# A planned attention and scan kernel on one core: idle matmuls, longer GpSimd pieces, another rule for late fills, and new seeds

## The chip, the cores and the metric

The kernel runs on one core of a Trainium2 chip. Its engines each follow a list of instructions of their own and meet at semaphores: TensorE (PE) multiplies matrices into eight PSUM banks of 128x512 fp32, ScalarE (ACT) evaluates functions, VectorE (DVE) and GpSimd (POOL) do elementwise work, and SyncE (SP) issues most of the transfers. The metric is the device time of one execution in microseconds (us); smaller is better.

## The reference

Two layers of 2048 tokens by 640 channels, their outputs side by side (2048 x 1280, bf16):

```python
# A: a diagonal complex state space model
Lam = Lambda_re + 1j * Lambda_im;  dt = exp(log_dt);  Lam_bar = exp(dt * Lam)
B_bar = ((Lam_bar - 1.0) / Lam)[:, None] * Bmat
Bu = einsum("bld,pd->blp", x, B_bar)
for t in range(L):  h = Lam_bar * h + Bu[:, t]
y = 2.0 * einsum("blp,dp->bld", hseq, Cmat).real + x * Dskip
# B: attention, 32 heads of 20 channels that share one key and one value head
q = heads(x @ wq);  k = x @ wk;  v = x @ wv
p = softmax(q k^T * 20 ** -0.5)
out = merged(p v) @ wo
```

## The kernel before

**Attention.** The work is cut into 32 groups: 4 blocks of 512 queries by 8 groups of four heads. A group has 4 heads x 16 blocks of 128 keys, so 64 *units*; a unit is a block of 128 keys by 512 queries of one head, and there are 2048 of them. For each unit PE multiplies keys with queries into one PSUM bank (a *fill*, `QK`), an engine takes the exponential, and PE multiplies the result with the values and adds it to the group's sums in the bank PV (`pv`). Sums leave PV at the end of a group by a VectorE copy (`raw_op`, line 1307, tile OTr). Softmax's denominator is a column of ones among the values; it divides later, in `dense_ops` on GpSimd and, for the last two groups, in `norm_last`.

**Two engines for the exponential.** ACT takes tiles of three or two units: PSUM tile R0 has three banks, R1 two, and fills alternate between them, so even tiles are mostly three wide and odd ones two (`ex_op`, line 1263, output P). VectorE takes single units, the *D units*: `dx_op` (line 1269) turns scores into the bits of a bf16 number by an addition to int16 (tile Pd), and `sh_op` (line 1274) makes three shifted copies of it, for up to three units at a time; the average of four shifted versions comes near to the exponential. A D unit's scores lie in one of two banks B0 and B1, which it shares with all background work, or in the third bank of R0 (named R0c), which is lent to it; then the even tile is two wide.

**Background work** is given in threads of operations: the queries of later blocks (`qt`), the state space model (`sa` the products B x and their rotation, `su` and `sr` the scan and its rotation on GpSimd and VectorE, `sy` the output y), the constants of C (`sc`), the normalisation (`dense`), and the output projection (`proj`). In `sc`, lines 852 to 862: per block of C's rows, GpSimd multiplies in five pieces of 128 columns into the fp32 buffer ctmp (line 858), twice, and VectorE makes CGre and CGim of it (line 860).

**The planner.** No order is written out by hand: `main` builds it when the program is made, from a clock per engine and an estimated duration per operation. In each step it collects candidates (a fill, an exponential, a D unit, a shift, a `pv`, the head of each thread), takes the one that would begin first, with a bias and some noise, and appends it to the list of its engine with the waits that it needs. Fill n may be placed once fill n - 2's exponential is placed. A background or `pv` operation on PE that would end later than the next fill could begin, plus an allowed lateness, is put behind the fill:

```python
t_fill = p.begin("pe", o.reads, o.writes)
t_fill = (t_fill, t_fill + self.after[n % 2])
...
if t < t_fill[0] and tl + o.occ * self.pace(tl) + 0.106 * (o.kind != p.pe_kind) > t_fill[1]:
    k = max(k, t_fill[0] + 0.01)
```

`self.after` is a pair: a short lateness of 0.1 to 0.2 us and a long one of 0.35 to 0.5. Where PE would idle for more than SPARE inside a group and has been thinly used, the planner puts in matmuls that add zeros to PV (kind `zero`, from the tile cs). The planner counts matmuls at double time when PE's use over the last 3.4 us is under COLD (`pace`, `load`).

**Seeds.** The units are cut into 64 turns, and at each turn `vary` draws a dozen parameters (among them `after`, the limits for D units, and noise) from the random generator with that turn's seed in SEEDS. So a change of an estimate or a seed gives another order from there on.

**The start.** `setup` loads x transposed, makes the rotation tables and the keys, and leaves a list `rest` on which `main` begins: VectorE's copies of keys 1024 to 2047 from the B banks (tiles KT), the value projection on PE into PV (80 matmuls), and VectorE's copies into VP. No `pv` may be placed before `rest` is empty; fills and exponentials may. `owner` says which thread holds each B bank.

Of the kernel before, what the change touches and what calls it, by code (L numbers as in the profile page):

```python
# [9 lines left out]
ALU = mybir.AluOpType  # L10
# [233 lines left out]
class _Kernel:  # L244
# [7 lines left out]
    QUOTA = 16  # L252
    AGE = 4.0
    DLAST = 58
    SPARE = 0.33
    WINDOW, BUSY, COLD = 3.4, 0.46, 0.36

    SLACK, SLOW = dict(dve=0.15, pool=1.0), dict(pool=1.0)
# [3 lines left out]


    TURNS = 64
    SEEDS = (19006, 20002, 21006, 22006, 23001, 24003, 25001, 26002, 27008, 28003, 0, 30006, 31008, 32005, 33006,
# [4 lines left out]

    def __init__(self, nc, t):
        self.nc, self.t = nc, t
# [544 lines left out]
    def scan_ops(self):  # L817

        K, NC = self, self.NC
        sc, NGRE, NGIM, GRE, GIM = K.sc, self.NGRE, self.NGIM, self.GRE, self.GIM  # L820
        t = self.t
# [11 lines left out]
        ct = [f"tm{i}{h}" for i in (4, 5, 6) for h in self.PIECES]  # L833
# [18 lines left out]
        for c in range(NC):  # L852
            cr, ci = K.Craw[c][:, 0, :], K.Craw[c][:, 1, :]
            keys = [f"Craw{c}0", f"Craw{c}1", "sc"] + (["ostage0", "ostage1"] if c == 4 else ws)
            for (dst, x, y, gx, gy, op, nm) in ((K.CGre, cr, ci, GRE, GIM, ALU.subtract, "CGre"),
                                                (K.CGim, ci, cr, NGRE, NGIM, ALU.add, "CGim")):
                for i in range(0, 640, 128):
                    pool(lambda e, y=y, c=c, gy=gy, i=i: e.tensor_scalar(K.ctmp[:, i:i + 128], y[:, i:i + 128], sc[:, gy, c:c + 1],  # L858
                                                                         None, op0=ALU.mult), keys, [f"ct{i}"] + ct * (i == 0), 128)
                dve(lambda e, dst=dst, x=x, op=op, c=c, gx=gx: e.scalar_tensor_tensor(  # L860
                    out=dst[:, c, :], in0=x, scalar=sc[:, gx, c:c + 1], in1=K.ctmp, op0=ALU.mult, op1=op),
                    keys + ct + [f"ct{i}" for i in range(0, 640, 128)], [nm], 695)
# [264 lines left out]
    def main(self):  # L1127
        K, p = self, self.p
# [8 lines left out]
        begun = [[False] * 4 for _ in range(NG)]  # L1137
# [4 lines left out]
        tiles = deque()  # L1142
# [21 lines left out]
        rest = self.rest  # L1164
# [4 lines left out]
        threads = [("rest", rest), ("norm", norm), ("dense", dense), ("proj", proj), ("qt", qt), ("qr", qr), ("sy", sy), ("sa", sa), ("su", su), ("sr", sr), ("sc", sc_), ("sx", sx), *fins]  # L1169
        owner = ["rest", "rest", None]  # L1170
        rest[-1].done = lambda: owner.__setitem__(slice(0, 2), [None, None])
        holds, since = {}, {}

        def bank(o):

            f = [i for i in range(2) if owner[i] is None]
            if not f:
                return None
            return min(f, key=lambda i: p.begin("pe", (), (f"B{i}",)))
# [50 lines left out]
        def want_d(g, t, n_tile, lent=False):  # L1230
            if not (g > 0 or taken[g] >= 24) or d_group(g) is None:
                return False
            if dunit_left.get(cur["d"] - self.DUNITS, 0):
                return False
            if lent:
                return (self.lend < 9 and owner[2] is None and t_left() and backlog(t) <= self.backlog - 0.5 * n_tile - self.lend
                        and p.begin("pe", (), ("R0c",)) <= t + self.spared[n_tile])
            if bank(None) is None:
                return False
            if any(owner[:2]) and any(t - x > self.starved[name] * (name != "qt" or len(self.qsent) > 0) for name, x in since.items()):  # L1240
                return False
            return (backlog(t) <= self.backlog - 0.5 * n_tile
                    and p.begin("pe", (), (f"B{bank(None)}",)) <= t + self.spared[n_tile])
# [68 lines left out]
        while True:  # L1312
            if self.units * self.TURNS // NU > turn:
                turn = self.units * self.TURNS // NU
                self.vary(self.SEEDS[min(turn, self.TURNS - 1)])
            cand = []
# [4 lines left out]
            def offer(kind, o, bias, thread=None, arg=None):  # L1321
                cand.append((p.begin(o.eng, *o.keys(), o.accum) + bias + self.noise * self.rng.random(), len(cand), kind, o, thread,
                             arg))

            t_fill = None
            early = bool(rest) and any(self.NKC - len(x) >= 8 for x in left[0])
            if cur["fill"] < cur["act"] + 2 and any(x < 64 for x in taken) and not early:
                n = cur["fill"]
                g = next(i for i in range(NG) if taken[i] < 64)
                if g in qt_done:  # L1330
                    t = p.begin("pe", (), (f"R{n % 2}",))
                    size, x = self.TILES[n % 2] - (n % 2 == 0 and owner[2] is not None), bank(None)
                    d = want_d(g, t, n % 2)
                    if not d and size == 3 and want_d(g, t, 0, True):
                        size, d, x = 2, True, 2
                    out, d = pick(size, d)
                    o = fill_op(n, out, d, x)
                    t_fill = p.begin("pe", o.reads, o.writes)
                    t_fill = (t_fill, t_fill + self.after[n % 2])
                    offer("fill", o, -self.noise, arg=(out, d, x))  # L1340
                    t = p.clock["pe"]
                    if d is None and want_d(g, t, 2):
                        d = pick(0, True)[1]
                        if d:
                            offer("fill", fill_op(n, [], d, bank(None)), 0.2, arg=([], d, bank(None)))
            full = bool(tiles) and tile_left.get(tiles[0][0] - self.PTILES, 0) > 0
            if tiles:
                n, out = tiles[0]
# [4 lines left out]
            if shifts:  # L1353
                o = sh_op(*shifts[0])
                t = p.begin(o.eng, *o.keys()) + p.PRE["dve"]
# [4 lines left out]
            if g < NG and g <= cur["raw"] and not rest:  # L1360
                n, whole = ready(g)
# [8 lines left out]
            for name, th in threads:  # L1370
                if not th:
                    continue
                o = th[0]
# [6 lines left out]
                if o.lock:  # L1380
                    i = bank(o)
# [19 lines left out]
            if t_fill is not None:  # L1401
                for i, (k, m, kind, o, name, arg) in enumerate(cand):
                    if o.eng == "pe" and (kind != "fill" or not arg[0]):
                        t = p.begin("pe", *o.keys(), o.accum)
# [4 lines left out]
            _, _, kind, o, name, arg = min(cand, key=lambda x: x[:2])  # L1409
# [4 lines left out]
            if o.eng == "pe":  # L1414
                g, t = cur["pv"], p.begin("pe", *o.keys(), o.accum)
                while (g < NG and any(begun[g]) and any(due[g]) and t - p.clock["pe"] > self.SPARE
                       and self.load(t) < self.BUSY):
                    self.go(self.mms([self.m1(K.PV[:, :], zeros, K.cs[:, 0, 0, :], False, False)],
                                     ["VP", "cosT"], ["PV"], accum=True, kind="zero"))
            self.go(o)  # L1420
            if kind == "bg":
                th = dict(threads)[name]
# [8 lines left out]
            elif kind == "fill":  # L1431
                out, d, x = arg
                self.units += len(out) + (d is not None)
                if out:
                    n = cur["fill"]
# [14 lines left out]
            elif kind == "ex":  # L1450
                n, out = tiles.popleft()
# [17 lines left out]
            elif kind == "sh":  # L1469
                us, i = shifts.popleft()  # L1470
# [60 lines left out]
```

## Time and profile before

| what | value |
|---|---|
| runs | 769.84, 770.16, 772.17 us (median 770.16) |
| the profiled execution | 770.28 us, of which the span from first to last instruction is 768.6 |
| ACT, line 1263 | 677 instructions, 733.1 us busy |
| DVE, line 1269 | 363 D units from the B banks 245.5 us, 73 from R0c 49.9 us |
| DVE, line 1274 | 513 shifts, 260.2 us |
| PE, line 421 (all matmuls) | 704.8 us |
| POOL, line 858 | 50 pieces, from 75.8 to 161.1 us |
| HBM | 9.21 MB read, 12.69 MB written: 28 GB/s over the span |

How to read it: all matmuls are recorded by one helper, so all have line 421, and tiles tell them apart: `R<-QT,KT` and `B<-QT,KT` are fills, `PV<-P,VP` and `PV<-Pd,VP` the products with the values, `PV<-WO,xbT` the value projection, `R<-WO,OTd` and `R<-WO,OTp` the last output projections. The record of an exponential begins while the one before still ends, so durations of one kind sum to more than the time in which ACT was busy. Busy times of PE are modelled.

### The profile page before, as it was taken

Reading aid. Unit: us, or ns where it says so; the run is one execution under the profiler, and the core shown is the slowest. Engines: PE = TensorE matmul, PEld = TensorE weight load, DVE = VectorE, ACT = ScalarE, POOL = GpSimd, SP = SyncE. Lnnn points to the kernel's source line nnn. Section 1 sums busy time; section 2 is a strip of 40 time slices with the busy share of each in tenths; the row PEclk is TensorE's granted clock in tenths of the full one; section 3 lists DMA queues with packets and bytes.
Section 4 is the critical chain, followed back from the end, with each engine's and each line's share of the span. In section 5 each row is a group of like instructions: output and inputs, shape, how many; then the busy total and the mean of one; then the engine's idle time right before and its main releaser. Section 6 shows DMA issues by size and latency. Waiting matters only on the chain.

```text
span 768.6 us, 16664 instructions
## 1 busy us (share of the span) xinstructions
PE 704.8 (92%) x6538; PEld 213.4 (28%) x6538; DVE 708.3 (92%) x1236; ACT 752.5 (98%) x710; POOL 446.0 (58%) x867
## 2 busy tenths in 40 slices
PE   5799988888889999998889999988889999889998
PEld 2222222222222333322223323322223332223333
DVE  5599999999998999999997999999999789999986
ACT  8999999999999999999999999999999999999995
POOL 5612354579989931088997300199986469990040
PEclk9899999899999999999999999999999999999999
DMA  9366301000021100220002100040000201000020
GB/s 186 57 143 134 74 16 49 8 24 14 3 51 30 42 8 27 56 60 15 15 9 67 42 23 9 23 93 10 15 15 28 66 33 34 14 15 17 18 61 35
DMA packets 61179, 31.50 MB, mean 41 GB/s; under 512 B 41510, under 2 KB 61102, under 8 KB 61102
## 3 DMA queue, kind: packets, MB, share of 16 engines
q1 hardware_dynamic: 59606, 30.14, 15.9%
q8 instruction: 52, 0.85, 0.5%
q10 hardware_dynamic: 1496, 0.30, 0.2%
q14 instruction: 25, 0.20, 0.1%
HBM read 9.21 MB, written 12.69 MB: 28 GB/s over the span
## 4 chain that ended last, share of the span: by engine, by line
ACT 74%; PE 15%; DVE 9%; POOL 1%; DMA 1%; issue 1%; ACTq 0%; DVEq 0%; POOLq 0%
ACT P L1263 72%; PE R L421 5%; PE PV L421 5%; PE B L421 4%; DVE Pd L1274 4%; DVE Pd L1269 3%; DVE hh L928 1%; DVE tm L901 1%; POOL tm L858 1%; DMA WO<-in_B_wk_dram 1%; ACT cs L691 1%; ACT Pd L690 0%; ACT KT L538 0%; DVE CGre L860 0%; ACT L503 0%
## 5 line engine op out<-in xcount | busy, mean ns | idle before, releaser
L1263 ACT ACTIVATE P<-R 128x1024 bf16<-128x1024 f32 (+1 forms) x677 | 733.1, 1354 | 4.3 <-PE R L421 1.8
L421 PE MATMUL R<-QT,KT 32*128 32x512 bf16 (+1 forms) x1685 | 266.9, 389 | 48.6 <-ACT P L1263 37.1
L1269 DVE TENSOR_SCALAR Pd<-B 128x512 int16<-128x512 f32 x363 | 245.5, 682 | 19.4 <-PE B L421 17.0
L1274 DVE TENSOR_SCALAR Pd<-Pd 128x1536 int16<-128x1536 int16 (+2 forms) x513 | 260.2, 541 | 0.4
L421 PE MATMUL PV<-Pd,VP 128*32 128x512 bf16 x1744 | 256.9, 386 | 2.0 <-DVE OTr L1307 1.0
L421 PE MATMUL PV<-P,VP 128*32 128x512 bf16 x1612 | 253.3, 389 | 0.7 <-DVE OTr L1307 0.6
L917 POOL TENSOR_TENSOR tm<-hh,cs 128x128 bf16<-128x128 f32 x320 | 163.9, 533 | 17.7 <-DVE hh L928 8.3
L421 PEld LDWEIGHTS R<-QT,KT 32*128 32x128 bf16 (+1 forms) x1685 | 66.1, 91 | 301.0 <-ACT P L1263 271.0
L421 PE MATMUL B<-QT,KT 32*128 32x512 bf16 x363 | 141.0, 389 | 0.0
L917 POOL TENSOR_TENSOR uh<-tm 128x128 bf16<-128x128 bf16 x160 | 81.0, 527 | 97.6 <-DVE tm L901 93.7
L917 POOL TENSOR_TENSOR W<-tm 128x128 bf16<-128x128 bf16 x160 | 93.5, 608 | 49.4 <-PE B L421 45.3
L421 PEld LDWEIGHTS PV<-Pd,VP 128*32 128x32 bf16 x1744 | 60.1, 94 | 65.7 <-issue 40.5
L421 PEld LDWEIGHTS PV<-P,VP 128*32 128x32 bf16 x1612 | 58.1, 94 | 58.8 <-issue 46.6
L1011 POOL TENSOR_TENSOR OTd<-OTd,rwide 128x128 bf16<-128x128 bf16 x80 | 33.2, 443 | 60.0 <-DMA OTd<-o_rows 58.2
L1269 DVE TENSOR_SCALAR Pd<-R 128x512 int16<-128x512 f32 x73 | 49.9, 683 | 3.0 <-PE R L421 2.4
L901 DVE TENSOR_TENSOR tm<-B,cs 128x1024 bf16<-128x1024 f32 x40 | 48.5, 1213 | 1.0 <-PE B L421 0.6
L858 POOL TENSOR_SCALAR tm<-W,sc 128x128 f32<-128x128 bf16 x40 | 32.3, 821 | 27.5 <-DVE CGre L860 15.9
L421 PE MATMUL B<-CGre,W 128*128 128x384 bf16 (+1 forms) x160 | 46.4, 305 | 0.0
L421 PE MATMUL B<-CGim,W 128*128 128x384 bf16 (+1 forms) x160 | 45.5, 299 | 0.0
L928 DVE TENSOR_TENSOR_SCAN hh<-sc,hini,uh 128x512 f32<-128x512 f32 x30 | 40.7, 1358 | 0.0
L421 PEld LDWEIGHTS B<-QT,KT 32*128 32x128 bf16 x363 | 32.9, 91 | 0.0
L421 PE MATMUL B<-xaT,BTre 128*128 128x512 bf16 x100 | 30.1, 384 | 0.1
(149 smaller groups left out, 437.2 us busy)
## 6 DMA issues: line engine op xcount, KB each, us to landing
o_rows<-OTr SPq DMA_DIRECT2D x32, 128.0 KB, 1.7
QT<-q_rows SPq DMA_DIRECT2D x30, 128.0 KB, 2.2
q_rows<-Qd SPq DMA_DIRECT2D x16, 160.0 KB, 2.9
OTd<-o_rows SPq DMA_DIRECT2D x16, 160.0 KB, 3.4
out_dram<-ystage SPq DMA_DIRECT2D x16, 160.0 KB, 1.9
out_dram<-ostage SPq DMA_DIRECT2D x12, 160.0 KB, 1.8
P<-in_B_wq_dram SPq DMA_DIRECT2D x1, 800.0 KB, 5.6
WO<-in_B_wo_dram SPq DMA_DIRECT2D x4, 200.0 KB, 3.4
```

Source lines behind the costliest of these rows:

```text
L421: ins = e.matmul(o() if callable(o) else o, lhsT=l, rhs=r, start=st, stop=sp, skip_group_check=True, **kw)
L691: act(lambda e, c=c, b=b: e.activation(K.cs[:, c, :, :].rearrange("p i n -> p (i n)"), K.tri[:, 4 * b + 2:4 * b + 4, :].rearrange("p r n - ...
L858: pool(lambda e, y=y, c=c, gy=gy, i=i: e.tensor_scalar(K.ctmp[:, i:i + 128], y[:, i:i + 128], sc[:, gy, c:c + 1], None, op0=ALU.mult), key ...
L901: dve(lambda e, k=k, h=h: e.tensor_tensor(K.tm[:, 2 * k:2 * k + 2, :], bass.AP(tensor=K.BB, offset=512 * int(h.key[1]), ap=[[512 * self.BA ...
L917: put(lambda e, c0=c0, end=end: e.tensor_tensor(out[:, c0:end], a[:, c0:end], b[:, c0:end], op), reads, [writes + h], n, gate=None if i el ...
L928: dve(lambda e, ri=ri, ini=ini: e.tensor_tensor_scan(K.hh[:, ri, :], dec, K.uh[:, ri, :], ini, ALU.mult, ALU.add), ["sc", *(f"uh{ri}{h}" f ...
L1011: ops.append(Op("pool", lambda e, c=c, m=m: e.tensor_tensor(K.OTd[:, m, c], K.OTd[:, m, c], K.rwide[:, c], ALU.mult), rw + [f"OTe{dd}" for ...
L1263: return Op("act", lambda e: e.activation(dst, K.R[n % 2][:, 0:512 * size], ACT.Exp, scale=self.exp_scale), [f"R{n % 2}"] + ["R0c"] * (siz ...
L1269: return Op("dve", lambda e: e.tensor_scalar(K.Pd[:, 0, u, :], K.B[x][:, :], self.d_off, 0.0, op0=ALU.add, op1=ALU.max), [key], [f"Pd{u}_0 ...
L1274: return Op("dve", lambda e: e.tensor_scalar(K.Pd[:, i, a:b, :], K.Pd[:, 0, a:b, :], float(self.SHIFTS[i]), 0.0, op0=ALU.subtract, op1=ALU ...
```

## The change

Four edits. In the changed file lines from 1172 on stand two further down, and by the end six.

1. Once the planner has placed VectorE's two copies out of the first B bank (`rest[1]`), and until a `pv` of group 0 is placed, a gap of PE over 0.25 us before the next operation is filled with matmuls into B0 that nobody reads (128 rows, 512 columns), as long as PE's use is under WARM = 0.8.
2. The estimate of a GpSimd piece of line 858 goes from 128 to 216 elements in `n / 450 + 0.1`.
3. The allowed lateness of a fill is the long one if the last tile that is filled but whose exponential isn't placed has three units, and the short one otherwise; before, it went by odd or even n.
4. All 64 seeds are new.

```diff
-    SPARE = 0.33
+    SPARE, WARM = 0.33, 0.8
...
-    SEEDS = (19006, 20002, 21006, 22006, 23001, 24003, 25001, 26002, 27008, 28003, 0, 30006, 31008, 32005, 33006,
+    SEEDS = (4007, 5006, 0, 0, 8006, 9003, 10005, 11001, 0, 13004, 14002, 15006, 16001, 17002, 18005, 19003,
...
                     pool(lambda e, y=y, c=c, gy=gy, i=i: e.tensor_scalar(K.ctmp[:, i:i + 128], y[:, i:i + 128], sc[:, gy, c:c + 1],
-                                                                         None, op0=ALU.mult), keys, [f"ct{i}"] + ct * (i == 0), 128)
+                                                                         None, op0=ALU.mult), keys, [f"ct{i}"] + ct * (i == 0), 216)
...
         rest[-1].done = lambda: owner.__setitem__(slice(0, 2), [None, None])
+        self.still = False
+        rest[1].done = lambda: setattr(self, "still", True)
...
-                    t_fill = (t_fill, t_fill + self.after[n % 2])
+                    t_fill = (t_fill, t_fill + self.after[bool(tiles) and len(tiles[-1][1]) == 3])
...
+                if self.still and not any(begun[0]) and owner[0] in (None, "rest") and "B0" not in o.keys()[1]:
+                    while t - p.begin("pe", (), ("B0",)) > 0.25 and self.load(t) < self.WARM:
+                        self.go(self.mms([self.m1(K.B[0], K.ident[:, :], K.xbT[:, 0, 0:512], True, True)], ["ident", "xbT0"], ["B0"],
+                                         kind="zero"))
             self.go(o)
```

The order that comes out, by its instructions (all others are as many as before):

| instruction | before | after |
|---|---|---|
| ACT P<-R, 1536 / 1024 / 512 wide | 258 / 419 / 0 | 263 / 416 / 1 |
| DVE Pd from B / from R0c | 363 / 73 | 357 / 69 |
| DVE shifts, 1536 / 1024 / 512 wide | 354 / 87 / 77 | 363 / 66 / 62 |
| PE R<-QT,KT / B<-QT,KT | 1685 / 363 | 1691 / 357 |
| PE PV<-P,VP / PV<-Pd,VP | 1612 / 1744 | 1622 / 1704 |
| PE PV<-cs,VP (zeros) | 72 | 62 |
| PE B<-xbT,ident (idle matmuls) | 0 | 7 |

8 rows, old and new, of the table SEEDS are left out of this document.

## The prediction

> **What bounds the kernel now.** I read the page first: busy shares, the clock row and the chain that ended last.
>
> ```profile
> span 768.6 us, 16664 instructions
> ...
> PE 704.8 (92%) x6538; PEld 213.4 (28%) x6538; DVE 708.3 (92%) x1236; ACT 752.5 (98%) x710; POOL 446.0 (58%) x867
> ...
> PEclk9899999899999999999999999999999999999999
> ...
> ACT 74%; PE 15%; DVE 9%; POOL 1%; DMA 1%; issue 1%; ACTq 0%; DVEq 0%; POOLq 0%
> ```
>
> ScalarE (ACT) is busy for 98% of the span and carries 74% of the chain; TensorE and VectorE have some 60 us idle each. So I looked at ACT's groups with their shapes kept apart, and at what ACT waited for.
>
> ```profile
> L1263 ACT ACTIVATE P<-R 128x1024 bf16<-128x1024 f32 x419 | 457.8, 1189 | 1.1 <-PE R L421 0.7 <-PE B L421 0.2
> L1263 ACT ACTIVATE P<-R 128x1536 bf16<-128x1536 f32 x258 | 418.3, 1621 | 3.2 <-PE R L421 1.2 <-PE B L421 1.1 <-PE PV L421 0.6
> ...
> ACT W L1101 <- PE R L421: 5.5, 2, 4.9
> ```
>
> The 677 exponentials of line 1263 take 1612 units (blocks of 128x512 scores): 419x2 + 258x3. The other 436 of the 2048 units are made by VectorE (363 + 73 in its rows of line 1269). The two rows sum to more than the page's 733.1 us because successive exponentials overlap. From start to start, the median is 904 ns after a 1024-wide one and 1331 after a 1536-wide one; the smallest are 904 and 1330. The first starts at 21.7 us, the last ends at 759.0. Its 418 + 258 successions at the smallest pitch would take 418x0.904 + 258x1.330 = 721.0 us; they take 736.3. The excess over the pitch sums to 15.1 us, 5.3 before 160 us and 9.8 from there to 760. This excess, of which the idle column shows only 4.3 (the overlap hides the rest), is all that a better order can win between the first and the last exponential.
>
> Where the excess has a cause that the change names, the table of stretches shows it.
>
> ```profile
> 24.80:28.20 3.40, 0.88 (x7) 0.19 (x5) 2.76 (x10) 3.40 (x3) 2.96 (x6) 1.00 0.33 90
> 28.20:31.60 3.40, 3.19 (x12) 0.65 (x12) 0.00 (x0) 3.40 (x5) 2.01 (x10) 0.50 0.03 5
> 31.60:35.00 3.40, 3.40 (x19) 0.56 (x17) 1.38 (x3) 2.78 (x3) 0.19 (x1) 0.50 0.06 3
> ...
> 137.40:140.85 3.45, 2.06 (x30) 0.58 (x27) 2.93 (x7) 3.45 (x4) 2.24 (x5) 1.00 0.00 0
> 140.85:147.70 6.85, 6.82 (x40) 1.34 (x44) 6.02 (x13) 5.73 (x6) 2.57 (x4) 0.50 0.07 23
> ```
>
> After each stretch's length come the busy times of PE, weight loads, DVE, ACT and POOL; the number after POOL's is the granted clock. Twice a stretch with a thinly used PE (0.88 and 2.06 us) is followed by one at half clock; a third, shorter one follows 1.93 us of 3.40 at 117. In the first, ACT loses 0.87 us (starts at 32.8 and 34.4); around the second, 1.83 us (141.5 to 147.4). What thinned PE before the second is in the timeline:
>
> ```profile
> 139.19 0.89 DVE L860 SCALAR_TENSOR_TENSOR CGre<-W,sc,tm 128x640 bf16<-128x640 bf16 x1 [0.52 <-POOL tm L858]
> ...
> 140.83 0.61 PE L421 MATMUL R<-QT,KT 32*128 32x512 bf16 x3 [0.81 <-DVE Pd L1269]
> ```
>
> VectorE waits 0.52 us for a GpSimd piece of line 858, its next unit is late, and PE waits 0.81 us for the bank that unit holds. Last, the end of the span:
>
> ```profile
> 764.27 0.43 PE L421 MATMUL R<-WO,OTd 128*128 128x320 bf16 x2
> ...
> 764.54 0.71 PE L421 MATMUL R<-WO,OTp 128*128 128x320 bf16 x4
> ...
> 765.28 0.70 ACT L1101 ACTIVATE W<-R 128x640 bf16<-128x640 f32 x1 [0.65 <-PE R L421]
> 766.02 0.38 ACTq L404 DMA_DIRECT2D out_dram<-W  x1
> ```
>
> Six projection matmuls, then ACT's copy, then the last store: this chain is serial.
>
> **The split between ScalarE and VectorE.** The new seeds give another order. In its instruction lists ACT has 416 exponentials of 1024, 263 of 1536 and one of 512: 1622 units; VectorE has 357 + 69 = 426. Ten units go to the engine that bounds. At the pitches, 416x0.904 + 263x1.330 = 725.9, and the last, 512 wide, about 0.59 (the shortest 1024-wide took 1.02, less half of 0.86): 726.5, against 721.0 + 1.02 = 722.0. That is **+4.4 us**, on the path. The two rows alone give the same: 1621 - 1189 = 432 ns per unit, and (733.1 - 1612x0.432)/677 = 54 ns per instruction, so 4.32 + 0.16. VectorE is spared 10 units of 0.68 (245.5 + 49.9 over 436), and its shifted copies change by +9 of 608 ns, -21 of 450 and -15 of 323: some 16 us in means of its rows, all off the path, since VectorE already has 60 us to spare. It counts for nothing, unless its lateness now causes stalls (first rival).
>
> **The end.** In the new order 12 matmuls, not 6, stand between the last four of the B banks and ACT's last copy (8 with OTd, 4 with OTp). The eight OTd matmuls at 762.1 took 0.97 us, 0.12 each: **+0.7 us**. The five new projection matmuls ahead lie under VectorE's copy of the last sums (0.69 us, line 1307) where eight others lay before. The extra 0.49 us copy of line 1061 fits in the 0.58 us that VectorE waited there. If not covered these cost 0.2 each.
>
> **Idle matmuls.** Seven 128x512 matmuls are put between the 13 fills after the value projection. Each holds PE 0.21 us (two B matmuls from wqd ended 0.21 apart) inside gaps of 1.23, 0.52 and 0.95 us, in which PE waits for ACT anyway; the bank they write is free by then, and only fills are queued behind them. Cost 0; if a gap were missing, 7x0.21 = 1.5. Three or four fall into the first thin stretch and raise 0.88 by 0.39 each, to some 2.1 to 2.4 us of 3.4. Stretches of 1.93 and 2.06 lost the clock, one at 530 us with 0.64 of its length busy (2.2) kept it: likely enough, not sure. Bounds of the gain: 0 to 0.9; I take **-0.9**. VectorE's 5.2 us wait at 28 us for the next query block should shrink too; ACT is not held by it.
>
> [...]
>
> **GpSimd's pieces.** Fifty multiplications of line 858 were planned with 128 and now with 216 elements in n/450 + 0.1: 0.38 and 0.58 us, where the trace has a median of 605 ns (40 pieces) and 837 (the last ten), and single ones up to 2627. Nothing is added or removed, only the planner places what waits for them later. The gain is bounded by what that lateness cost: 0 to 1.8 us; longer pieces are still under-rated, but they waited on VectorE only once for over 0.5 us, so **-1.8**. It is delivered if VectorE and PE get other work in those places, which the order has: the ten sums of lines 860 and after are spread over units 34 to 94, where they were over 32 to 84.
>
> **Lateness by the tile in work.** The allowed lateness of a fill no longer goes by odd or even but by whether ACT has a 1536-wide tile still ahead. Stricter cases are odd tiles after a 1024-wide even one; they cost 1.6 us in 80 successions. Stricter also means that PE leaves a gap instead of doing background work, to be paid later. Bounds -1.6 to +1.6; I take 0.
>
> **The rest of the excess**, 15.1 - 0.9 - 1.8 = 12.4 us: most of what is after 160 us falls at the ends of the 32 groups (0.70 at 395, 0.50 at 580, 0.47 at 652), where sums are copied out and tiles are narrow. The new order has as many groups and the same planner there. Between successive fills PE's work (0.21 per group of four, 0.32 per fill, 0.11 per change of kind, as the timeline's starts show) exceeds ACT's pitch by over 0.4 us 63 times, before 50 times; those 50 had 87 ns excess on average. That would be +1.1; pairs of fills over 2.5 us fall from 5 to 1, which speaks the other way. I take 0.
>
> **Sum.** The profiled execution took 770.28 us (768.6 of span and 1.7 around it), close to the median of 770.16. 770.28 + 4.4 + 0.7 - 0.9 - 1.8 = 772.7: slower by 0.33%.
>
> **Rivals.** (1) Faster: the stalls at ends of groups halve, because VectorE, with 10 units less, frees its banks earlier and PE stops waiting there. Then 9.8 becomes 4.9 and the lateness edit gives its 1.6: 772.7 - 6.5 = 766.2. It decides from 4.9 us on (time before less 0.3%). For it: 19.4 us of VectorE's waits were for PE, idle fillers of PV fall from 72 to 62, overfull pairs. Against: PE's fills waited on VectorE only 3.2 us in all (8 times), so only that much is surely its doing. (2) None of the named recoveries comes: the clock falls elsewhere for some 7 us, as it did at 120 and 141, and the 63 overfull places cost their 1.1: 770.28 + 5.1 + 1.1 = 776.5. For it: pieces of up to 2627 ns are planned at 580. Against: the planner counts clock and port. (3) Little: as forecast, and the lateness edit gives 1.6: 771.1, no change that this measurement can tell (within 0.3%, 2.3 us).
>
> **Chances.** Forecast 0.45 (own range 770.5 to 775), rival 1 0.18, rival 2 0.24, rival 3 0.13. The forecast's own range lies about one third under 772.5. Faster by over 0.3%: 0.19, rival 1 and a little of 3; within: 0.29; slower: 0.52. The range 766 to 778 leaves out the far ends of rivals 1 and 2.
>
> **What would show it.** ACT's rows must read 416, 263 and 1; line 1263's busy time some 737. The clock row's second digit should be 9, with VectorE's wait for Qabs under 3 us; line 860's wait on GpSimd gone. ACT's last copy waits some 0.7 longer. The forecast is wrong if the excess over pitch is under 8 us or over 18, wherever it then falls.

## The result and the profile after

The changed kernel takes 776.9 us (median; 776.16 to 777.53), the kernel before beside it 769.84: a ratio of 1.0095, 95% interval 1.0075 to 1.0115. A fifth execution of the changed kernel, 1899.3 us at a whole clock, stands alone and is left out of that span. The changed kernel is slower, by 7 us where the prediction had 2.5. That is within the whole range (766 to 778) but above the forecast's own (770.5 to 775), and it is the figure of the second rival (776.5), not of the forecast (772.7). The profiled execution took 776.9 us. The lines of its page that answer to those shown of before:

```profile
span 775.2 us, 16577 instructions
...
PE 706.4 (91%) x6505; PEld 213.0 (27%) x6505; DVE 702.6 (91%) x1199; ACT 757.4 (98%) x713; POOL 435.1 (56%) x867
...
PEclk9799999889999999999999999999999999999999
...
ACT 76%; PE 11%; POOL 6%; DVE 5%; issue 1%; DMA 0%; ACTq 0%; POOLq 0%
```

ACT is 4.9 us busier (757.4 against 752.5) in a span 6.6 us longer, and its share of the chain rose from 74% to 76%. The second digit of the clock row, which the idle matmuls should have raised from 8 to 9, is 7. ACT's groups with their shapes kept apart (line, form, count | busy us, mean ns | idle before):

```profile
L1265 ACT ACTIVATE P<-R 128x1024 bf16<-128x1024 f32 x416 | 456.7, 1191 | 0.4 <-PE R L421 0.2
L1265 ACT ACTIVATE P<-R 128x1536 bf16<-128x1536 f32 x263 | 426.4, 1621 | 5.5 <-PE R L421 3.0 <-PE B L421 2.2
...
L1101 ACT ACTIVATE W<-R 128x640 bf16<-128x640 f32 x2 | 1.4, 704 | 6.2 <-PE R L421 6.2
```

The counts are the ones read from the order. The mean durations are as before (1191 and 1621 ns, 1189 and 1621 there), so each exponential costs what it did; there are more wide ones, and their idle time went from 3.2 to 5.5 us. The last copies' idle time went from 5.5 to 6.2. From the starts of the exponentials both spans can be cut without remainder:

| us | before | after | difference | forecast |
|---|---|---|---|---|
| start of the first exponential | 21.68 | 21.63 | 0.0 | 0 |
| all exponentials at their pitch, with the last one's duration | 722.3 | 726.8 | +4.5 | +4.4 |
| excess over the pitch | 15.1 | 16.7 | +1.6 | -2.7 |
| of it 20 to 40 us | 1.9 | 3.1 | +1.2 | -0.9 |
| 40 to 160 us | 3.3 | 2.6 | -0.7 | -1.8 |
| 160 to 760 us | 9.8 | 10.9 | +1.1 | 0 |
| from the last exponential's end to the end | 9.5 | 10.1 | +0.6 | +0.7 |
| span | 768.6 | 775.2 | +6.6 | +2.4 |

(The pitch is 904 ns after a 1024-wide exponential and 1330 after a 1536-wide one, as in the prediction; the 512-wide one is the last, so none follows it.) Both terms that count work held. What failed are the recoveries. The table of stretches of the profile after shows how the clock went (from:to, length, then busy us of PE, weight loads, DVE, ACT and POOL, then the granted clock):

```profile
18.20:21.70 3.50, 1.84 (x11) 0.46 (x9) 2.83 (x6) 3.17 (x10) 1.89 (x3) 1.00 0.09 31
21.74:25.15 3.41, 3.41 (x87) 2.40 (x85) 3.16 (x5) 2.25 (x2) 3.35 (x3) 0.50 0.66 145
25.15:28.57 3.42, 3.36 (x14) 0.67 (x11) 2.24 (x9) 2.89 (x3) 2.84 (x7) 0.50 0.16 45
28.57:31.98 3.41, 3.35 (x11) 0.55 (x9) 0.00 (x0) 2.95 (x3) 1.53 (x9) 0.50 0.06 5
141.20:144.62 3.42, 2.08 (x19) 0.49 (x16) 3.42 (x6) 3.42 (x5) 0.84 (x2) 1.00 0.02 5
144.62:151.45 6.83, 6.62 (x51) 1.24 (x52) 5.34 (x11) 6.16 (x6) 2.77 (x5) 0.50 0.06 20
165.10:168.51 3.41, 2.02 (x22) 0.48 (x22) 3.33 (x7) 3.41 (x4) 0.00 (x0) 1.00 0.27 88
168.51:175.34 6.83, 6.65 (x50) 1.31 (x50) 5.74 (x11) 5.91 (x7) 3.93 (x5) 0.50 0.05 16
```

Three thinly used stretches (1.84, 2.08, 2.02 us), each followed by half clock: 10.2 + 6.8 + 6.8 = 23.9 us, against 17.1 before. The first thin stretch lies before the idle matmuls can begin; what they then do is in the timeline (start us, us, engine, line, out<-in, count, idle time before it):

```profile
25.10 0.61 PE L421 MATMUL B<-xbT,ident 128*128 128x512 bf16 x1
...
25.22 2.37 ACT L1265 ACTIVATE P<-R 128x1536 bf16<-128x1536 f32 x2 [1.22 <-PE R L421]
...
26.18 1.27 PE L421 MATMUL B<-xbT,ident 128*128 128x512 bf16 x2
...
27.39 0.61 PE L421 MATMUL R<-QT,KT 32*128 32x512 bf16 x3
27.55 0.35 DVE L581 COPY wq<-P 128x400 bf16<-128x400 bf16 x1
...
28.04 2.36 ACT L1265 ACTIVATE P<-R 128x1536 bf16<-128x1536 f32 x2 [0.46 <-PE R L421]
```

The clock was already halved at 21.74. PE is therefore no longer idle here (3.36 of 3.42 us). The idle pair of 26.18 lasts 1.27 us in the record, the three fills behind it start at 27.39, and ACT waits for them. VectorE's wait for Qabs, which should have shrunk from 5.2 us to under 3, is 5.1 (2.9 in the control below, where the clock was whole here). At 141 the thin stretch has another cause than before. PE's rows there:

```profile
141.65 0.39 PE L421 MATMUL R<-QT,KT 32*128 32x512 bf16 x3 [0.20 <-ACT P L1265]
...
142.57 0.39 PE L421 MATMUL R<-QT,KT 32*128 32x512 bf16 x2 [0.20 <-ACT P L1265]
...
143.91 0.39 PE L421 MATMUL R<-QT,KT 32*128 32x512 bf16 x3 [0.62 <-ACT P L1265]
144.83 0.61 PE L421 MATMUL R<-QT,KT 64*128 64x512 bf16 x2 [0.53 <-ACT P L1265]
```

Nothing is late: PE waits for ACT, the engine that bounds, and its list has no work to do between these fills. PE is used for 2.08 of 3.42 us, half clock follows, and then ACT waits for PE: 0.67 us at 150.04 in the timeline, for matmuls into a B bank. The wait on GpSimd's pieces is gone, as foreseen. The rows of line 860 (duration min/median/max in ns, first and last start) list nothing that it waited for:

```profile
L860 DVE SCALAR_TENSOR_TENSOR CGre<-W,sc,tm x4: 872/876/879, 90.8 to 147.6; 128x640 bf16<-128x640 bf16 x4
...
its engine sat idle before it (us, times) until:
who waited for it (us, times):
```

Last, ACT's rows at the end of the timeline:

```profile
769.79 0.70 ACT L1101 ACTIVATE W<-R 128x640 bf16<-128x640 f32 x1 [4.73 <-PE R L421]
771.96 0.70 ACT L1101 ACTIVATE W<-R 128x640 bf16<-128x640 f32 x1 [1.47 <-PE R L421]
```

The second copy waits 1.47 us, before 0.65: the twelve matmuls of 1.25 and 0.71 us between them.

### The profile page after: what moved, and what is told of

Its sections match the earlier page's. It is cut to its first block, busy times and chain, and to the rows that moved or that the text cites. A ratio compares the mean times of both kernels' runs of the same rounds, so it can differ in the third digit from the quotient of the medians.

```text
span 775.2 us, 16577 instructions
## 1 busy us (share of the span) xinstructions
PE 706.4 (91%) x6505; PEld 213.0 (27%) x6505; DVE 702.6 (91%) x1199; ACT 757.4 (98%) x713; POOL 435.1 (56%) x867
## 4 chain that ended last, share of the span: by engine, by line
ACT 76%; PE 11%; POOL 6%; DVE 5%; issue 1%; DMA 0%; ACTq 0%; POOLq 0%
ACT P L1265 74%; PE R L421 4%; PE PV L421 4%; PE B L421 3%; POOL tm L917 3%; DVE Pd L1276 2%; POOL uh L917 2%; DVE Pd L1271 2%; POOL W L917 1%; DVE tm L901 1%; ACT cs L691 1%; DVE hh L928 0%; ACT Pd L690 0%; DMA WO<-in_A_Lambda_im_dram 0%; ACT KT L538 0%
## 5 line engine op out<-in xcount | busy, mean ns | idle before, releaser
L1271 DVE TENSOR_SCALAR Pd<-B 128x512 int16<-128x512 f32 x357 | 241.6, 683 | 27.6 <-PE B L421 24.2
L1276 DVE TENSOR_SCALAR Pd<-Pd 128x1536 int16<-128x1536 int16 (+2 forms) x486 | 254.6, 558 | 1.0
L421 PE MATMUL B<-QT,KT 32*128 32x512 bf16 x357 | 139.2, 390 | 0.0
L917 POOL TENSOR_TENSOR W<-tm 128x128 bf16<-128x128 bf16 x160 | 85.2, 553 | 68.4 <-PE B L421 64.5
L1011 POOL TENSOR_TENSOR OTd<-OTd,rwide 128x128 bf16<-128x128 bf16 x80 | 35.7, 473 | 78.8 <-DMA OTd<-o_rows 76.9
L1271 DVE TENSOR_SCALAR Pd<-R 128x512 int16<-128x512 f32 x69 | 47.0, 682 | 5.4 <-PE R L421 4.9
L858 POOL TENSOR_SCALAR tm<-W,sc 128x128 f32<-128x128 bf16 x40 | 28.0, 712 | 35.8 <-DVE CGre L860 23.3
```

The costliest lines, as they stand in the source:

```text
L421: ins = e.matmul(o() if callable(o) else o, lhsT=l, rhs=r, start=st, stop=sp, skip_group_check=True, **kw)
L917: put(lambda e, c0=c0, end=end: e.tensor_tensor(out[:, c0:end], a[:, c0:end], b[:, c0:end], op), reads, [writes + h], n, gate=None if i el ...
L1011: ops.append(Op("pool", lambda e, c=c, m=m: e.tensor_tensor(K.OTd[:, m, c], K.OTd[:, m, c], K.rwide[:, c], ALU.mult), rw + [f"OTe{dd}" for ...
L1271: return Op("dve", lambda e: e.tensor_scalar(K.Pd[:, 0, u, :], K.B[x][:, :], self.d_off, 0.0, op0=ALU.add, op1=ALU.max), [key], [f"Pd{u}_0 ...
L1276: return Op("dve", lambda e: e.tensor_scalar(K.Pd[:, i, a:b, :], K.Pd[:, 0, a:b, :], float(self.SHIFTS[i]), 0.0, op0=ALU.subtract, op1=ALU ...
```

## The experiments

Two theories. **A:** ScalarE bounds, and time follows its units and the excess; the excess that the recoveries were to remove is not tied to the things named (idle PE at 25 us, GpSimd's pieces), so removing them moves it. **B:** the loss is the clock's: 24 us at half clock instead of 17, and a kernel with a whole clock would show no loss. Ratios are to the kernel before, run beside on the same chip; times are medians, with the lowest and highest.

| kernel | us | ratio, 95% interval |
|---|---|---|
| after, again | 775.41 (773.16 to 778.89) | 1.0088, 1.0061 to 1.0115 |
| after, idle matmuls 4 columns wide | 774.77 (773.30 to 776.62) | 1.0073, 1.0054 to 1.0092 |
| after, ten units fewer on ScalarE | 772.84 (770.11 to 775.91) | 1.0049, 1.0033 to 1.0065 |
| after, kept warm | 782.68 (780.04 to 783.64) | 1.0163, 1.0140 to 1.0186 |
| after, more spins | 774.68 (773.23 to 778.36) | 1.0063, 1.0038 to 1.0087 |
| after, seeds of before | 789.90 (787.37 to 794.01) | 1.0260, 1.0227 to 1.0294 |
| before, more spins | 769.34 (767.17 to 771.66) | 1.0002, 0.9990 to 1.0014 |
| before, seven idle matmuls | 770.83 (767.65 to 773.51) | 1.0014, 0.9999 to 1.0029 |
| before, ten units more on ScalarE | 774.99 (773.58 to 776.12) | 1.0076, 1.0061 to 1.0090 |
| before, short pieces | 769.30 (767.99 to 770.70) | 0.9999, 0.9990 to 1.0009 |
| before, more spins and idle matmuls | 769.77 (768.17 to 772.47) | 0.9998, 0.9982 to 1.0014 |
| before, seeds of after | 791.48 (791.03 to 792.05) | 1.0278, 1.0249 to 1.0307 |

### After, again

No edit: the control for the others. 

> The changed kernel once more, as the control of this group. Theory: 1.0095 of the kernel before, within 0.2%; its profile again shows 10 units more on ScalarE (737.9 us busy in line 1265), but the stretches at half clock may begin at other places than 21.7, 144.6 and 168.5 us, because they begin on a grid of 3.41 us that differed between the two profiles (28.2 there, 21.7 here). Rival: the places are the same, and the order alone sets them.

Measured 1.0088 (1.0061 to 1.0115). Its profiled execution had a span of 772.4 us, 2.8 less than the first, and an excess of 14.4. The same order ran into other stretches of half clock:

```profile
18.20:21.70 3.50, 1.96 (x18) 0.66 (x17) 2.83 (x6) 3.50 (x9) 0.74 (x2) 1.00 0.26 89
21.74:25.15 3.41, 3.25 (x84) 2.24 (x81) 2.74 (x8) 2.62 (x3) 3.35 (x4) 1.00 0.79 185
25.15:28.57 3.42, 2.78 (x14) 0.78 (x14) 1.95 (x5) 3.42 (x4) 3.13 (x5) 1.00 0.02 5
...
143.49:146.90 3.41, 3.35 (x27) 0.73 (x27) 2.81 (x5) 3.18 (x4) 1.11 (x2) 0.50 0.00 0
...
163.97:167.38 3.41, 3.25 (x26) 0.67 (x26) 3.37 (x6) 3.41 (x4) 1.01 (x2) 0.50 0.25 82
```

Here the clock was whole when the idle matmuls began, they raised the stretch at 25 us to 2.78 us of use, the clock stayed, and the excess from 20 to 40 us was 0.9 (before 1.9, in the first profile after 3.1). So here the idle matmuls did what they are for; where the clock had fallen at 21.7 already, they did not. One profile is not enough to read a term of 1 us from: between these two of the same kernel that stretch differs by 2.2 us.

### Idle matmuls of four columns

```diff
-  self.go(self.mms([self.m1(K.B[0], K.ident[:, :], K.xbT[:, 0, 0:512], True, True)], ["ident", "xbT0"], ["B0"],
-                   kind="zero"))
+  idle = self.mms([self.m1(K.B[0], K.ident[:, :], K.xbT[:, 0, 0:512], True, True)], ["ident", "xbT0"], ["B0"],
+                  kind="zero")
+  idle.fn = lambda e: e.matmul(K.B[0][:, 0:4], lhsT=K.ident[:, :], rhs=K.xbT[:, 0, 0:4], start=True, stop=True,
+                               skip_group_check=True)
+  self.go(idle)
```

> The changed kernel in the same order, but the seven idle matmuls write 4 columns, not 512. Theory A (they cost time: they stand before fills, and at half clock each holds PE for 0.43 us): faster than the changed kernel by 1 to 2 us (0.2%). Theory B (they keep the clock up, as forecast): slower by up to 1 us. Theory C (hidden either way): within 0.3 us.

Measured 1.0073 (1.0054 to 1.0092), 0.15% under the control with intervals that overlap: unclear. In its profile the clock had again fallen early (half from 22.9 us for 10.2), and the excess from 20 to 40 us was 2.8. So at half clock that stretch is expensive even when the idle matmuls are short; how much of it they cause at their full width is not separated.

### Ten units fewer on ScalarE

Ten exponentials of 1536 stop after 1024; the kernel leaves out the exponential of ten units.

```diff
+  cut = size == 3 and n % 58 == 10
+  end = 512 * (size - cut)
-  return Op("act", lambda e: e.activation(dst, K.R[n % 2][:, 0:512 * size], ACT.Exp, scale=self.exp_scale),
+  return Op("act", lambda e: e.activation(dst[:, 0:end], K.R[n % 2][:, 0:end], ACT.Exp, scale=self.exp_scale),
```

> The changed kernel in the same order, but ten of the 1536-wide exponentials are made 1024 wide, so ten units are left out (their products then use what the buffer held before). Theory A (ScalarE bounds, and the ten units that moved to it cost 0.43 us each): 4.3 us less than the changed kernel, 0.55%. Theory B (PE and the ends of groups bound, ScalarE is only as late as they are): under 1.5 us less.

Measured 1.0049 (1.0033 to 1.0065): 2.6 us under the control, where ten units at the pitch are 4.3. Its groups of ACT:

```profile
L1267 ACT ACTIVATE P<-R 128x1024 bf16<-128x1024 f32 x426 | 459.8, 1181 | 0.4 <-PE R L421 0.2
L1267 ACT ACTIVATE P<-R 128x1536 bf16<-128x1536 f32 x253 | 406.7, 1608 | 5.5 <-PE R L421 3.1 <-PE B L421 1.8
```

The counts moved by ten, the idle column hardly. The excess rose to 17.3 us (14.4 and 16.7 in the two profiles after), but only at the start, which met half clock from 22.2 us: 3.6 us from 20 to 40, and 13.7 outside that stretch, where the two profiles after have 13.5. So the profile shows no new waiting elsewhere. To take the clock out, lines were laid through time against mean granted clock of the executions, with one slope for both groups: at equal clock the difference to the control is still 2.5 us (1.9 to 3.1). Theory B gave less than 1.5, so A is nearer; the units pay, but downward not in full, and why not stays open.

### Ten units more on ScalarE

Onto the order of before; an extra exponential of 512 columns, whose output nobody reads.

```diff
+  if kind == "ex" and tiles[0][0] % 66 == 20:
+      p.add("act", lambda e: e.activation(K.wq1[:].rearrange("p c n -> p (c n)")[:, 0:512], K.R[0][:, 0:512], ACT.Exp,
+                                          scale=self.exp_scale), ["R0"], ["wq1"], False, 0.0, 0.0)
```

> The kernel before in its own order, with ten more exponentials of 512 columns on ScalarE, spread over the run, whose results nobody reads. Theory A (ScalarE bounds throughout): 10 x (0.427 + 0.05) = 4.8 us more. Theory B (ScalarE is held up by fills often enough to hide a part, as the ten units left out of the changed kernel gave back 2.6 of 4.3 us): 2 to 3.5 us more.

Measured 1.0076 (1.0061 to 1.0090), +5.8 us (4.7 to 6.9); at equal clock, by such lines, +4.9 (4.4 to 5.4). The next exponential starts 477 to 495 ns after each extra one, so ten of them are 4.8 to 4.9. Its rows (the extra exponentials are line 1421):

```profile
L1263 ACT ACTIVATE P<-R 128x1024 bf16<-128x1024 f32 x419 | 459.6, 1197 | 0.9 <-PE R L421 0.7 <-PE B L421 0.2
L1263 ACT ACTIVATE P<-R 128x1536 bf16<-128x1536 f32 x258 | 420.3, 1629 | 3.0 <-PE B L421 1.5 <-PE R L421 0.8 <-PE PV L421 0.5
L1421 ACT ACTIVATE wq<-R 128x512 bf16<-128x512 f32 x10 | 8.0, 803 | 0.0
```

Nothing takes them up: ACT's idle time stays as it was (0.9 and 3.0 us, before 1.1 and 3.2), and the time goes up by what the ten take on ScalarE. ScalarE bounds, and ten units on it are enough by themselves for the larger part of the change's loss.

### Kept warm

To the order of after: the five matmuls that spin at 18 us (idle matmuls of the kernel before, ahead of the first scores) are issued twice, and in two stretches every `pv` operation, of up to four matmuls, is followed by a matmul that adds zeros.

```diff
-  go(self.mms([self.m1(K.R[0][:, 0:512], K.wk4[:, 0, :], K.xbT[:, 0, 0:512], True, True)],
-              ["wk4", "xbT0"], ["R0"], accum=True))
+  o = self.mms([self.m1(K.R[0][:, 0:512], K.wk4[:, 0, :], K.xbT[:, 0, 0:512], True, True)],
+               ["wk4", "xbT0"], ["R0"], accum=True)
+  if n == 5:
+      one = o.fn
+      o.fn = lambda e, one=one: (one(e), one(e))[1]
+  go(o)
...
+  if kind == "pv" and any(begun[cur["pv"]]) and sum(due[cur["pv"]]) > 4:
+      t = p.begin("pe", *o.keys(), o.accum)
+      if any(a < t < b for a, b in ((134.0, 148.0), (156.0, 173.0))):
+          o.fn = lambda e, f=o.fn: (f(e), e.matmul(K.PV[:, :], lhsT=zeros, rhs=K.cs[:, 0, 0, :], start=False, stop=False,
+                                                   skip_group_check=True))[1]
```

> The changed kernel in the same order, with more use of PE that nobody needs: five more idle matmuls before the first scores (at 18 us), and one matmul that adds zeros to PV after each product with the values in two stretches, about 139 to 153 and 161 to 178 us; 44 rows more in all. Theory A (the stretches at half clock cost what ScalarE loses in and just behind them: 3.1 + 1.5 + 1.2 us): 3 to 5 us less than the changed kernel, and the clock stays whole there. Theory B (the order itself is late there: too much work between fills): no gain, or 1 us more.

Measured 1.0163 (1.0140 to 1.0186), 7 us over the control, although the clock of the profiled execution (780.04 us) was whole throughout:

```profile
span 778.3 us, 16597 instructions
...
PEclk9999999999999999999999999999999999999999
```

Its excess was 1.0 us from 20 to 40, but 4.6 from 40 to 160 and 4.7 from 160 to 200 (2.1 and 1.1 in the control). The matmuls that kept the clock cost more than the half clock they prevented; that they do so by standing in front of fills is the likely reading. The second theory of this section, that a kernel with a whole clock would show no loss, falls in this form: at this price a whole clock does not bring the loss back.

### More spins, seven idle matmuls, and both, on the order of before

The first has the first part of the diff above. The second puts 1 or 2 idle matmuls ahead of fills, seven in all, at no cost to the planner, so that all else keeps its order. The third has both.

```diff
+  if kind == "fill" and arg[0]:
+      for _ in range({2: 1, 3: 1, 4: 2, 5: 1, 6: 2}.get(cur["fill"], 0)):
+          p.add("pe", lambda e: e.matmul(K.B[0], lhsT=K.ident[:, :], rhs=K.xbT[:, 0, 0:512], start=True, stop=True,
+                                         skip_group_check=True), ["ident", "xbT0"], ["B0"], False, -0.01, 0.16, None, p.pe_kind)
```

> The kernel before in its own order, with five more idle matmuls at 18 us, before the first scores (the five that stand there are issued twice). Theory A (stretches at half clock between 21 and 35 us cost ScalarE there): the clock stays whole up to 28 us at least, the excess over pitch between 20 and 40 us falls from 1.9 to about 1.0 us, and the median is 0.3 to 1 us under the kernel before. Theory B (the order of that stretch sets it): no change of the excess, within 0.3 us.

> The kernel before in its own order, with the seven idle matmuls of the change added at the same fills (one, one, two, one and two before the fills 2 to 6), and nothing else. Theory A (they hold the clock, as forecast): 0.5 to 0.9 us less than before. Theory B (at half clock they hold up the fills behind them, and they come too late to prevent it): 0.5 to 1.5 us more. Theory C: within 0.3 us.

> The kernel before in its own order with both: five more idle matmuls at 18 us and the seven of the change. Alone, the first changed nothing and the second cost 0.1%. Theory A (together they hold the clock, and a whole clock saves the excess of 20 to 40 us): excess there 1.0 us, not 1.9, and 0.5 to 1 us less than before, so below both kernels. Theory B: within 0.3 us of before, or slower by 1.

Measured 1.0002 (0.9990 to 1.0014), 1.0014 (0.9999 to 1.0029) and 0.9998 (0.9982 to 1.0014). The spins alone did not keep the clock: it was half from 24.8 us for 10.2, and the excess from 20 to 40 us was 1.9 as before. With both it was whole there and the excess 1.2. The idle matmuls alone, forecast at -0.9 us, give +1.1 (-0.1 to +2.2). The stretches of the profile with idle matmuls alone:

```profile
18.20:21.60 3.40, 1.73 (x10) 0.45 (x8) 2.73 (x5) 3.00 (x8) 1.53 (x3) 1.00 0.12 43
21.60:25.00 3.40, 3.40 (x86) 2.35 (x84) 3.24 (x6) 2.31 (x2) 3.34 (x3) 0.50 0.55 112
25.00:28.40 3.40, 3.34 (x12) 0.62 (x9) 2.56 (x10) 2.75 (x3) 2.96 (x6) 0.50 0.27 78
28.40:31.80 3.40, 3.34 (x11) 0.62 (x10) 0.00 (x0) 2.94 (x3) 1.79 (x10) 0.50 0.03 6
```

It is the picture of the first profile after: use of 1.73 us before 21.6, half clock from there, the idle matmuls inside it, and an excess from 20 to 40 us of 3.1. Over all profiles with idle matmuls and single spins the start was at half clock in five (after, four columns, ten units fewer, seeds of before, this one) and whole in one (the control). With idle matmuls and doubled spins it was whole in all three (kept warm, more spins on after, both on before). Without idle matmuls it was half in all five (before, more spins, ten units more, short pieces, seeds of after), from between 23.5 and 28.2 us. So the two belong together; but even together they bring nothing that can be measured.

### More spins, on the order of after

The spins' three lines once more, here alone.

```diff
...
+  if n == 5:
+      one = o.fn
+      o.fn = lambda e, one=one: (one(e), one(e))[1]
...
```

> The changed kernel in its own order, with the five idle matmuls that stand at 18 us issued twice. With them ahead, and the change's seven behind the value projection, the profile with much added use of PE had a whole clock at 22 to 35 us and an excess of 1.0 us between 20 and 40 us; the changed kernel's own two profiles had 3.1 (half clock from 21.7 for 10.2 us) and 0.9 (whole clock). Theory A (the seven cost or gain by the clock that they meet): clock whole in that stretch, 0.5 to 2 us less than the changed kernel, and a smaller spread. Theory B (chance decides anyway): no difference.

Measured 1.0063 (1.0038 to 1.0087). Its profile has a whole clock at the start and an excess of 0.8 us there, 13.4 in all. The median is 0.25% under the control's, with overlapping intervals, and the spread is no smaller (773.2 to 778.4 us). By its ratio it is still some 5 us over the kernel before.

### Short pieces, on the order of before

GpSimd's pieces of line 858 on 16 of 128 columns, so that they are early whatever the planner thinks. The kernel leaves out seven eighths of the products that go into CGre and CGim; the buffer is zeroed once instead.

```diff
-  pool(lambda e, y=y, c=c, gy=gy, i=i: e.tensor_scalar(K.ctmp[:, i:i + 128], y[:, i:i + 128], sc[:, gy, c:c + 1],
+  pool(lambda e, y=y, c=c, gy=gy, i=i: e.tensor_scalar(K.ctmp[:, i:i + 16], y[:, i:i + 16], sc[:, gy, c:c + 1],
```

> The kernel before in its own order, with the GpSimd pieces of line 858 on 16 of their 128 columns (seven eighths of the products for CGre and CGim are left out), so that they are never late. Theory A (their lateness costs what was forecast): 1.5 to 2 us less than before, and no stretch at half clock at 141 us. Theory B (the ends of groups thin PE there anyway): within 0.5 us of the kernel before, and the excess over pitch from 140 to 160 us stays over 1 us.

Measured 0.9999 (0.9990 to 1.0009): nothing, where the prediction had -1.8 us. Its stretches, and below the dots those of the profile with ten units more on ScalarE, whose pieces have all their 128 columns:

```profile
116.72:120.13 3.41, 2.06 (x19) 0.50 (x17) 3.40 (x6) 3.41 (x4) 1.29 (x4) 1.00 0.03 10
120.13:126.96 6.83, 6.64 (x53) 1.36 (x49) 5.90 (x11) 5.83 (x6) 1.58 (x6) 0.50 0.49 129
137.40:140.85 3.45, 2.65 (x34) 0.62 (x26) 3.32 (x8) 3.45 (x4) 1.52 (x6) 1.00 0.00 0
140.85:147.70 6.85, 5.65 (x59) 1.56 (x59) 6.79 (x14) 6.85 (x8) 0.81 (x3) 1.00 0.07 23
...
119.06:125.89 6.83, 5.96 (x43) 1.32 (x43) 6.70 (x13) 6.83 (x7) 4.56 (x5) 0.50 0.46 123
137.40:140.85 3.45, 2.87 (x38) 0.74 (x34) 3.26 (x8) 3.45 (x4) 2.12 (x4) 1.00 0.00 0
140.85:147.70 6.85, 5.43 (x59) 1.57 (x59) 6.71 (x14) 6.85 (x7) 2.94 (x5) 1.00 0.07 23
```

With the pieces early, PE is used 2.65 us instead of 2.06 before 140.85, the clock stays whole, and the excess from 140 to 160 us falls from 1.9 to 0.1. At 120 the clock fell for 6.8 us, not 3.4, and the excess from 120 to 140 rose from 0.3 to 1.5; in all its profile has 14.6 us (before 15.1), and the median over twelve executions shows no gain at all. But the same picture comes with the pieces as they were. Of the five profiles of before's order with whole pieces, VectorE waits for one of them in two (before, 0.5 us, and more spins, 0.6), and these have half clock at 141 and 144 and an excess of 1.9 and 2.3 us from 140 to 160. In the other three (ten units more, idle matmuls, both) it waits for none, the clock is whole there, and that excess is 0.1. So the wait belongs to some executions and not to the order, and this experiment can't credit the change at 141 to the short pieces. What it shows is the median: without late pieces the kernel is no faster.

### The seeds exchanged

After's three other edits with before's seeds (the diff), and before's planner with after's seeds (the same diff the other way).

```diff
-    SEEDS = (4007, 5006, 0, 0, 8006, 9003, 10005, 11001, 0, 13004, 14002, 15006, 16001, 17002, 18005, 19003,
...
+    SEEDS = (19006, 20002, 21006, 22006, 23001, 24003, 25001, 26002, 27008, 28003, 0, 30006, 31008, 32005, 33006,
...
```

> The three edits of the planner with the seeds of before. Its order has 1628 units on ScalarE (266 of 1536, 415 of 1024), 16 more than before. Theory A (the number of units on ScalarE decides): 7 us more than before, 0.9%. Theory B (seeds and planner are fitted to each other, and an unfitted order also has a longer excess over pitch): 13 to 25 us more, 2 to 3%, with an excess over 25 us.

> The planner of before with the new seeds. Its order has 1625 units on ScalarE (264 of 1536, 416 of 1024, one of 512), 13 more than before. Theory A (units alone): 5.8 us more than before, 0.75%. Theory B (fitted seeds): 13 to 30 us more, 2 to 4%.

Measured 1.0260 (1.0227 to 1.0294) and 1.0278 (1.0249 to 1.0307): both 20 us slower than the kernel before. The orders have 1628 and 1625 units on ScalarE; at 0.43 these are 7 and 6 us of the 20. The excess of their profiles is 24.1 and 29.6 us, one stall of 5.1 us among it in the second. So a set of seeds fits one planner and was worth some 20 us in either case, and what the three edits do to the order can't be told from runs that keep the seeds. Counts of orders that were only planned, not run, say as much: over 40 sets of random seeds VectorE gets 420 to 423 units on average from before's planner, from the planner with one edit alone and from that with all three, with a standard deviation of some 4 within each. The 436 of before and the 426 of after are both above that; most of the ten units' difference lies in the seeds found, not in what the edits do to the planner.

## Why the prediction was right, and where it was not

- **The split, +4.4: right.** +4.5 in the two profiles; ten units added to the order of before cost 5.8 (4.7 to 6.9), ten taken from that of after gave 2.6. Two small errors cancel in it: the last exponentials, put at 1.02 and 0.59 us, took 1.27 and 0.91. (Before, the successions took 736.1 us, not 736.3; the excess of 15.1 is right.)
- **The end, +0.7: right.** +0.6, in the place named.
- **Idle matmuls, -0.9: wrong.** The step assumed a whole clock where they begin, as in the one profile of before, and a cost of 0 since "only fills are queued behind them". At half clock PE has no gap left to put them in (in the profile after it is busy for 3.36 of 3.42 us from 25.15), and the fills behind them are what ACT waits for (1.22 us before 25.22, 0.46 before 28.04). In the order of before they measure +1.1 (-0.1 to +2.2). In the order of after the excess from 20 to 40 us is 0.9 or 3.1 by the clock that the start meets. The whole clock up to 28.2 us was chance of the first profile: three others of before's order without idle matmuls are at half clock from 23.5, 24.6 and 24.8.
- **GpSimd's pieces, -1.8: wrong.** The step was "the gain is bounded by what that lateness cost", with the whole bound taken as gain. The bound was read from one execution, and the wait is not there in three of five profiles of the same order. It is gone in the profile after, and gone with short pieces, without gain in the time. Half clock comes all the same: around 120 us in before's order, with short pieces and with whole ones alike; in the order of after at 144.6 and 168.5, where PE waits for ACT (0.62 us before 143.91 and before 166.42) and nothing is late.
- **Lateness, 0: held, as far as it shows.** Odd tiles after a 1024-wide one have 1.5 us of excess (1.6 before). What the rule does to the choice of an order was only tried together with the other edits and seeds.
- **The rest of the excess, 0: too low by 1.1.** It is as much as the count that the prediction set aside would give (63 overfull places for 50, 87 ns each), but that these places cost it was not tried. The stretch from 160 to 760 us repeats well for an order, 9.8 to 10.0 us in five profiles of before's order; in four of after's order or near it, it is 9.9 to 11.4, so the 1.1 is of the size of that spread and not sure.
- **The balance.** The forecast's sum erred by 4.3 us of excess: 2.1 at the start, 1.1 between 40 and 160 us, 1.1 after. Rival 2 named the first two ("none of the named recoveries comes", the clock falls elsewhere), and its third part, the overfull places, is of the right size. So the direction came out by the two counted terms, while the size lay in the range only by the room left for rival 2. Rival 1, in which VectorE with ten units less frees its banks earlier, is out: what VectorE was spared went into waiting (its D units waited 24.2 us for PE at B banks, before 17.0), and the excess rose by 1.6 us in the profile.
- **The clock (theory B).** It goes with the spread, not with most of the loss. By lines through time against mean granted clock, with one slope, after's control is 6.3 us (5.7 to 6.8) over the kernel before at equal clock. One pair of profiles shows it more directly: both orders with idle matmuls and doubled spins, at clocks of 0.996 (after) and 0.998 (before). Their excess is nearly the same (13.4 and 13.6 us), and yet the spans are 771.5 and 766.5. These 5.0 us are, to 0.1, the two counted terms, 4.5 and 0.6.

What stays open: how the 2 us beyond the two counted terms divide between the clock and the order (at equal clock the lines leave 1.2 us to the order, the pair of profiles none); and whether the edits, with seeds sought as long as before's, would give a better order. That wasn't tried. No version among these beats the kernel before beyond its interval.

## What to carry to other kernels

Sum the work of the bounding engine first: ten units of 512 moved onto it set most of this result, and start-to-start times, not the idle column, show how little slack it has. A stall seen in one profile isn't a gain in the bank: see whether other executions of the same order have it, ask what limits the same stretch once it is gone, and try it alone (here by shortening the work, without touching the order) before crediting it. Work added to keep a clock whole belongs ahead of the moment at which it falls (here it then held in three profiles of three, with no gain that could be measured); added later, once the clock had fallen, it stood in front of the fills that ACT waited for (1.22 us at 25.22 in the profile after).

## What the hardware showed unexpectedly

**The same program meets different clocks.** Half clock comes in whole multiples of 3.41 us (3.4, 6.8 and 6.8 us in the profile of before, 10.2, 6.8 and 6.8 in the first of after), and where it begins changed with the execution: in the changed kernel at 21.7, 144.6 and 168.5 in the first profile, at 143.5 and 164.0 in the control. Mean clocks of single executions go from 0.979 to 0.993 before, and time follows: correlations of -0.89 to -0.95 in three groups of 17 to 29 executions, 3.6 to 5.1 us per 0.01. So 15.4 us at half clock (0.01 over a span of 769, half lost) go with 3.6 to 5.1 us more. The spread of 768 to 773 us is mostly this. In the first profile after, the clock fell behind stretches in which PE was used for 1.84, 2.08 and 2.02 us out of 3.4 to 3.5.

**The use that the trace records does not settle when the clock falls.** Within each of three profiles the falls lie on one grid of 3.41 us: 28.2, 120.4 and 140.8 us in before (27 and 6 steps apart), 21.7, 144.6 and 168.5 in after (36 and 7), 143.5 and 164.0 in the control (6). Among whole steps of that grid, 2.26 us of use lost the clock (ten units more, up to 119.06), and 2.18 kept it (before, 529.96 to 533.37). At the start, steps with 2.7 to 3.2 us of recorded use lost it in three profiles of before's order (ten units more, short pieces, more spins); 2.0 to 2.2 us of that use are the 80 matmuls of 20 columns of the value projection. So no threshold follows from recorded use, whose matmul ends are modelled, and how such short matmuls count for the clock is not shown.
